# A rebuilt instruction list for a fused attention and feed-forward block: a second mask area, new planned durations, and 117 moved units of work

## The chip, the cores and the metric

The kernel runs on one core of one Trainium2 chip, as one launch. The metric is the device time of that launch in microseconds (us). The core has a matrix engine, TensorE (PE in the profile, with its weight loads listed as PEld), and four others: VectorE (DVE), ScalarE (ACT), GpSimd (POOL) and SyncE (SP). Here SP issues nearly all transfers (DMAs). Every engine works through its own list of instructions in order. An instruction that waits holds up everything behind it on its engine.

## The reference

One transformer block over x[1, 2048, 448], in float32: a pre-LN attention with 16 heads of 28 and a sliding window of 256 keys, then a pre-LN GEGLU feed-forward. The biases and scales of the layer norms are not there.

```python
# attention
qkv = (layernorm(x) @ wqkv).reshape(B, S, 3, 16, 28)...   # q, k, v
scores = einsum("bhqd,bhkd->bhqk", q, k) * 28 ** -0.5
mask = (i - j >= 0) & (i - j < 256)                      # query i, key j
p = softmax(where(mask, scores, -1e9))
h = x + (p @ v) @ wo
# feed-forward, F = 1792
g, u = layernorm(h) @ w_gate, layernorm(h) @ w_up
out = h + (gelu_tanh(g) * u) @ w_down
```

## The kernel before

**Precision.** Projections are computed from operands that are split in a high and a low part (`to_hi`, L435 on ACT; `to_lo`, L438 on DVE or POOL), with several matmul terms summed in PSUM: 11 per 128-row tile of q or k (`project_tile`, L683) and per value tile (`values`, L647), 6 per output tile (`output`, L1001).

**Attention.** The 2048 tokens are 16 tiles of 128. Attention is cut into 16 blocks B = 0 to 15: a block is one group of four heads (B % 4) by one chunk of 512 queries (B // 4). For a block the kernel does two passes over the scores. The first computes scores with queries on the partitions; DVE adds a mask to each piece and takes its maximum (L853). The 32 x 16 maxima of a block are turned on DVE (L883, L885), copied by ACT (L887) and written by four transfers into an extra row of q (`maxima`, L890), so that the second pass gives scores less their maximum. The second pass has keys on the partitions; ACT takes the exponentials (L859) and POOL zeroes what lies outside the window with `affine_select` (L865). Then comes the attention product (`attend`, L939), its scaling (`drain`) with the copies of oblk and ohl on ACT (L435), and the output product (`output`, L1001) with the addition to the residual on DVE (L1004).

PE's matmuls for the two passes are issued in `excursion`: a round of up to 64 small matmuls at a time, of the probabilities of one block, the maxima of another, or both in a row. Each such part writes four of the eight PSUM banks. Between rounds PE does projections, value products, output products, and at the end of attention the first matmuls of the feed-forward (L1243).

**Masks.** A 64-query half tile sees five blocks of 64 keys, of which the first is cut by the window and the last by the diagonal. Those of the first two tiles of the sequence see fewer. For these `tile_keys` returns the list of key blocks of each half and an offset into one mask buffer. Piece x of a tile is computed by one round and has its own mask columns.

**Layer norm and its transposed form.** Each tile is normalised by ACT (L492) into one of two buffers xn. Most tiles of the first norm are transposed on PE. For others, and in the second norm, `turn` transposes within 32 x 32 blocks on DVE (L537) and four SP transfers per tile (L540) carry the result to DRAM, for the first norm to xl and for the second to an xn area there. Its buffer xn in on-chip memory is the same for each of these tiles, so the next tile's transposition writes where these four transfers read. `turned` later loads and splits them.

**Feed-forward.** From about 324 us on a dense stream of half-array matmuls runs (`first` L1243, the gate and up products L1450, the down products L1526 and L1561), each with weight and token splits on ACT, DVE and POOL.

**What sets the order.** No loop order in the source is the order on the chip. Every piece of work is an `Op` of the class `Lists`: engine, cost, latency, a number `key`, what it reads and writes, PSUM banks. `Lists.run` walks through a modelled time. For each engine it looks at the pieces that could start first, within a few hundredths of a microsecond of each other, takes the one with the lowest key, and so appends to that engine's fixed list. The modelled latency of a transfer has an allowance MARGIN. Some elementwise operations have `alts`: the planner picks the engine (ACT or DVE, DVE or POOL) that would end first. So a change of a duration or key changes the orders of all lists, not what is computed.

```python
return min((f for f in found if f[3] <= t0), key=lambda f: (f[1].key, f[0]))[:3]
```

Of the kernel before, what the change touches and what calls it, by code (L numbers as in the profile page):

```python
# [23 lines left out]
BIG = 3.0e38  # L24
# [46 lines left out]
MARGIN = 0.7  # L71
# [24 lines left out]
WARM = 26.0  # L96

# [10 lines left out]
class Op:  # L108
    __slots__ = ("eng", "cost", "lat", "key", "fn", "deps", "users", "left", "banks", "port", "ready", "start", "fin",
# [10 lines left out]
class Lists:  # L120
# [3 lines left out]
    def __init__(self):  # L124
        self.ops, self.seen, self.open, self.all = [], {}, {}, {}
# [171 lines left out]
def block_kernel(ctx: ExitStack, tc, x, wqk_in, wv_in, wo_in, gu_in, rest_in, cw_in, down_in, out):  # L297
# [35 lines left out]
    pool.tile([128, 112], F32, name="pad2")  # L333
# [46 lines left out]
    kept = [m.rearrange("p (b r) -> p b r", r=12) for m in (v_m[:, 8 * VT:8 * VT + 96], mt[:, 512:608])]  # L380
# [59 lines left out]
    def dma(key, size, fn, r=(), w=(), cost=0.44, after=(), tag=None):  # L440
        return op("sp", cost, 0, key, fn, r, w, size=size, after=after, tag=tag)
# [10 lines left out]
    def layer_norms(ts, key, kind):  # L452
# [15 lines left out]

        for t in ts:
# [13 lines left out]
    def normalise(t, key, kind):  # L483
        moved = kind == "ln2" or t in TURNED
# [58 lines left out]
    def turned(t, key, kind):  # L543
        tc = col(t)
# [68 lines left out]
    def constants(after):  # L613
        def const_mask():
            nc.gpsimd.memset(mask, 0.0)
            nc.gpsimd.memset(mask[0:64, 320:384], -BIG)
            for h in HALF[:2]:
# [5 lines left out]
        op("pool", 1.0, 1.0, -18, const_mask, (), ["mask"], port=True, after=after)  # L623
# [7 lines left out]
    def wv_split(p):  # L631
        key = VHALF - 14 if p else WVKEY
# [7 lines left out]
    def values(t, p, n):  # L640
        key = 64 * (t // 4) + (VKEY if t < 12 else VLAST)[t % 4] if t > 3 else 8 * t - 37 if not p else VHALF + 6 * t
# [16 lines left out]
    def wqk_split(m):  # L658
        key = -34 + 3 * m if m < 4 else 6 * m - 28
# [10 lines left out]
    def project_tile(c, m):  # L670
        g, s = divmod(m, 2)
# [99 lines left out]
    def excursion(key, sf, pf):  # L771
        reads, work = [], []
# [49 lines left out]
        for n, (work, reads, writes, width, banks) in enumerate(steps):  # L822
# [3 lines left out]
            cost = width * 4 / 2400 + 0.012  # L826
            ops.append(op("pe", cost, cost + 0.2, key, lambda work=work, banks=banks: run(work, banks), rd, wr, held, tag="bin", mode=3))
# [4 lines left out]
        if sf is not None:  # L832
            banks = steps[-1][4]
# [3 lines left out]
        if pf is not None:  # L837
            width, banks = steps[0][3:]
            for j in range(4):
                probs(key, pf, width, j, banks[j])  # L840
            for G in new:
                select(G, key + 1)
# [31 lines left out]
    def maxima(B):  # L874
        g, u = B % 4, B % 2
# [44 lines left out]
    def attend(B):  # L920
        g, c = block(B)
# [23 lines left out]
        op("pe", cost, cost + 0.2, 16 * B + LAG_V, go, reads, (), banks, tag="att", mode=2)  # L945


    def drain(B):
        (bx, by), h = acc[B], B % 2
# [29 lines left out]
        for cost, fn, rd, wr in steps:  # L979
            cost *= 0.58 if last else 1  # L980
            op(name, cost, cost + 0.05, key + 1, fn, ["oblk", ("rcp", h), *rd], wr, port=True)
        op("dve", 0.625, 0.71, key + 2, lambda: nc.vector.transpose(oT, oblk), ["oblk"], [tok])
# [6 lines left out]
    def output(p, c):  # L989
        B = 4 * c + 2 * p + 1  # L990
        key = 16 * B + LAG_O
        for i in range(4):
            t = c * 4 + i

            k = Bank("last" if B == NB - 1 else "task")
            wk = key + (i if B == NB - 1 else 3 * i)
# [10 lines left out]
    def wo_weights(g):  # L1007
        p, h = divmod(g, 2)
# [94 lines left out]
    def tokens_x(cp, key, parts):  # L1103
# [788 lines left out]
```

## Time and profile before

| what | value |
|---|---|
| time, median of 3 runs | 698.02 us (697.04 to 699.13) |
| the profiled execution's own time | 699.35 us |
| its span (first to last instruction) | 697.6 us |
| granted TensorE clock, mean | 0.998 |
| bytes moved, mean rate | 69.69 MB, 100 GB/s |

The span runs from the first to the last instruction of one profiled execution, and the row of busy times gives each engine's part of it. In a row by stage, what follows the stretch is its length, then for each engine the busy time with the number of instructions that lie in it, then the clock that the throttle granted to TensorE, the share of the DMA engines' time, and the rate. In a row in order of time, the numbers are start and busy time of a group of equal instructions that follow each other, then the engine, the line in the source, the operation, what is written and read, the shape, the count, and in brackets how long the engine stood idle before and on which operation of which engine it waited. In a row of waits, the waiting operation stands left of the arrow and the releaser right, then the sum, the number and the longest of these waits. Matmuls overlap each other in the array, so the busy times of two neighbouring groups overlap by some hundredths of a microsecond.

### The profile page before, as it was taken

The page shows a single profiled execution, that of the slowest core. Times are in us where ns is not written, and L with a number is a line of the kernel's source. Part 1 is how long each engine was busy: PE and PEld are TensorE (multiplying, and loading weights), DVE is VectorE, ACT ScalarE, POOL GpSimd, SP SyncE. Part 2 cuts the span into 40 slices and gives each one's busy share as a digit, 9 for nine tenths or more (in the row PEclk, how much of TensorE's full clock was granted, in tenths as well). Part 3 has the DMA queues.
Part 4 walks back from the last instruction along what each step waited for, and adds up shares of the span by engine and source line. Part 5 has one row for each costly group of instructions (what it writes and reads, how often), then busy time and mean ns, then how long its engine had stood idle before and what let it go on. Part 6 is the DMA issues. An engine that isn't in the chain of part 4 may idle for free. (4 is left out here: it accounts for less than half of the span.)

```text
span 697.6 us, 22824 instructions
## 1 busy us (share of the span) xinstructions
PE 677.0 (97%) x9162; PEld 566.8 (81%) x9162; DVE 525.6 (75%) x1575; ACT 360.8 (52%) x788; POOL 204.6 (29%) x433
## 2 busy tenths in 40 slices
PE   8999999999999989999999999999999999999996
PEld 7887677777876777778988887888889889999885
DVE  8975678767678777638995899676757888887754
ACT  5656646654466464657553465544524544535430
POOL 5335554564546356670210120000000210111000
PEclk9999999999999999999999999999999999999999
DMA  8311211121312426233654666415103744443102
GB/s 306 86 36 40 41 31 55 21 51 31 90 23 55 113 63 216 68 93 110 148 103 128 208 174 193 119 46 142 59 14 119 222 133 132 136 143 86 43 14 106
DMA packets 67081, 69.69 MB, mean 100 GB/s; under 512 B 42528, under 2 KB 55008, under 8 KB 66400
## 3 DMA queue, kind: packets, MB, share of 16 engines
q1 hardware_dynamic: 66832, 68.13, 34.9%
q8 instruction: 71, 1.16, 0.7%
q14 instruction: 34, 0.28, 0.1%
q10 hardware_dynamic: 144, 0.11, 0.0%
HBM read 58.82 MB, written 22.45 MB: 116 GB/s over the span
## 5 line engine op out<-in xcount | busy, mean ns | idle before, releaser
L853 DVE CUSTOM_DVE_ANT_0 mt<-bank,mt 128x64 bf16<-128x64 f32 (+4 forms) x368 | 115.4, 373 | 25.3 <-PE bank L792 22.2
L1450 PE MATMUL bank<-xT,proj 64*128 64x512 f32 x645 | 120.7, 389 | 0.0
L865 POOL TENSOR_SCALAR_AFFINE_SELECT pp<-pp 64x256 f32<-64x256 f32 x240 | 95.9, 418 | 59.8 <-ACT pp L859 54.2
L1450 PE MATMUL bank<-xo,proj 64*128 64x512 f32 x456 | 98.4, 389 | 0.5 <-DVE e L1366 0.3
L859 ACT ACTIVATE pp<-bank 128x512 f32<-128x512 f32 x152 | 78.3, 597 | 24.7 <-PE bank L792 24.2
L1450 PEld LDWEIGHTS bank<-xT,proj 64*128 64x128 f32 x645 | 81.0, 184 | 9.2
L683 PE MATMUL bank<-xT 128*128 128x512 f32 x308 | 80.4, 403 | 2.9 <-ACT pp L859 2.6
L1526 PE MATMUL bank<-proj,gh 64*128 64x448 f32 x624 | 75.3, 363 | 0.3 <-ACT e L1365 0.2
L683 PEld LDWEIGHTS bank<-xT 128*128 128x128 f32 x308 | 55.4, 188 | 19.1 <-ACT pp L859 6.0
L1526 PEld LDWEIGHTS bank<-proj,gh 64*128 64x128 f32 x624 | 63.1, 185 | 6.4 <-ACT e L1365 1.2
L1450 PEld LDWEIGHTS bank<-xo,proj 64*128 64x128 f32 x456 | 59.5, 185 | 8.1 <-DVE e L1366 0.7
L1450 PE MATMUL bank<-xT,w 64*128 64x512 f32 x276 | 53.8, 390 | 0.3 <-DVE raw L1462 0.3
L792 PE MATMUL bank<-k,q 28*64 28x320 f32 (+4 forms) x1624 | 50.1, 331 | 2.2 <-ACT v L435 1.0
L1450 PE MATMUL bank<-xo,w 64*128 64x512 f32 x240 | 49.7, 391 | 0.9 <-DVE raw L1462 0.6
L1545 DVE TENSOR_TENSOR hres<-bank,hres 128x448 f32<-128x448 f32 (+1 forms) x85 | 47.0, 610 | 1.1 <-PE bank L1526 1.1
L647 PE MATMUL bank<-proj,xT 128*128 128x448 f32 (+1 forms) x220 | 44.3, 340 | 1.5 <-ACT pp L859 1.2
L792 PE MATMUL bank<-q,k 29*64 29x192 f32 (+4 forms) x1664 | 44.4, 327 | 0.3 <-DVE mx L853 0.3
L792 PEld LDWEIGHTS bank<-k,q 28*64 28x64 f32 x1624 | 37.3, 131 | 8.1 <-DVE mx L853 2.0
L792 PEld LDWEIGHTS bank<-q,k 29*64 29x64 f32 x1664 | 30.4, 131 | 15.8 <-issue 5.7
L647 PEld LDWEIGHTS bank<-proj,xT 128*128 128x128 f32 x220 | 35.7, 189 | 8.2 <-ACT pp L859 3.1
L939 PEld LDWEIGHTS bank<-pp,v 64*29 64x29 f32 x1664 | 32.1, 103 | 10.8 <-ACT pp L859 3.1
L939 PE MATMUL bank<-pp,v 64*29 64x192 f32 (+4 forms) x1664 | 39.4, 319 | 1.5 <-DVE mx L853 1.2
(197 smaller groups left out, 1297.5 us busy)
## 6 DMA issues: line engine op xcount, KB each, us to landing
gu<-in_gu_dram SPq DMA_DIRECT2D x18, 480.0 KB
proj<-gu SPq DMA_DIRECT2D x24, 288.0 KB
proj<-down SPq DMA_DIRECT2D x22, 224.0 KB
proj<-gu SPq DMA_DIRECT2D x24, 192.0 KB
hres<-in_x_dram SPq DMA_DIRECT2D x16, 224.0 KB
w<-gu SPq DMA_DIRECT2D x12, 288.0 KB
out_dram<-hres SPq DMA_DIRECT2D x15, 224.0 KB
xT<-xn SPq DMA_DIRECT2D x26, 128.0 KB
```

Source lines behind the costliest of these rows:

```text
L647: op("pe", mm(224 * n), 0.29 if n == 1 else 0.38, key + a / 16, lambda a=a, h=h, wb=wb, xb=xb: nc.tensor.matmul(bank[b.k][:, 0:224 * n], x ...
L683: op("pe", mm(512) + 0.002, 0.403, key, lambda a=a, h=h, wb=wb, xb=xb: nc.tensor.matmul(bank[b.k], wqk[m][:, h, wb, :], xT[:, xb, cc * 128 ...
L792: nc.tensor.matmul(bank[banks[j].k][dst, at:at + 64 * n], w, x, start=True, stop=True, tile_position=(32 * j, 64 * h), skip_group_check=True)
L853: nc.vector.tensor_tensor_reduce(junk[turn_of[0]][:, 0:x], bank[b.k][:, 64 * o:64 * o + x], mask[:, lo:lo + x], 1.0, -BIG, OP.add, OP.max, ...
L859: op("act", 0.065 + width * 0.00088, 0.16 + width * 0.00088, key, lambda: nc.scalar.activation(pp[:, j, at:at + width], bank[b.k][:, 0:wid ...
L865: nc.gpsimd.affine_select(a, a, pattern=[[0, 4], [-cm, 64]], compare_op=op_, fill=0.0, base=0, channel_multiplier=cm)
L939: nc.tensor.matmul(bank[banks[h].k][32 * j:32 * j + DH + 1, 64 * lo:64 * hi], v[HALF[h], at_v(4 * c - 2 + kh // 2), 4 * g + j, :], pp[HALF ...
L1450: nc.tensor.matmul(bank[b.k], w, xarea(u.cp, xl, xs, side)[:, xk], start=p in (1, 2, 5) and not k and not t, stop=t == 2, tile_position=(6 ...
L1526: nc.tensor.matmul(bank[banks[q].k][:, 0:D], h[oh][0]()[HALF[x], q * 128:q * 128 + 128], d[wh][0]()[HALF[x]], start=not ph and not y and n ...
L1545: op("dve", 0.07 + w * 0.463 / D, 0.163 + w * 0.463 / D, key, lambda: nc.vector.tensor_tensor(hres[:, t, c0:c0 + w], bank[b.k][:, c0:c0 + ...
```

## The change

**Keys of the first two tiles.** Before, the second half of tiles 0 and 1 had its list of key blocks rotated by one and shared the mask columns by an offset of 64. Now both halves have the same list in ascending order and start at offset 256, and a second diagonal area is added to the mask buffer (at 448 for the lower half, at 512 for the upper), which grows from 384 to 576 columns. Since the halves now agree, adjacent pieces of both can be made by the same matmuls: four score rounds of blocks 0 to 3 have 24 instead of 32 matmuls of their list (32 fewer in all, 1612 for 1644 on this side). The two junk areas move behind the larger mask, and the second half of `kept`, which had lain there, gets a tile of its own in place of the unused `pad2`.

**Planned durations.** In the planner's model MARGIN goes from 0.7 to 0.5, each transfer costs 0.1 more on SP, a score round's first part 0.06 and its last 0.02 in place of 0.012 on top of its columns and its latency 0.28 for 0.2, an attention product's latency 0.42 for 0.2, the mask's construction 1.6 for 1.0.

**Places.** Every unit of work gets a name (`L.unit`: ln for layer norms, x for score rounds, m for the maxima and p for the exponentials of a round, o for output products, q for projections, v for values, and so on), and a table PLACE of 117 entries adds a number to the key of each op of the unit.

No line of the computation changes apart from the first item. As all three change the planner's orders, instructions move on all engines; where an operation has a free choice, nine elementwise additions of the feed-forward go from DVE to POOL. PE has 6653 instructions for 6686, DVE 1569 for 1575, ACT 784 for 787, POOL 444 for 433, SP 558 for 558.

```diff
-MARGIN = 0.7
+MARGIN = 0.5
...
+PLACE = {
+    "k3": -17.1, "kv0": -31, "ln1.4": 18, "q0.0": 6, "kv1": -72, "v3.0": 77, "ln1.5n": 25, "q0.2": -37, "ln1.10": -54,
...
+}
...
-        o.eng, o.cost, o.lat, o.key, o.fn, o.port, o.size, o.tag, o.mode = eng, cost, lat, key, fn, port, size, tag, mode
+        o.eng, o.cost, o.lat, o.fn, o.port, o.size, o.tag, o.mode = eng, cost, lat, fn, port, size, tag, mode
+        o.key, o.unit = key + PLACE.get(self.unit, 0), self.unit
...
-    pool.tile([128, 112], F32, name="pad2")
+    kept_m = pool.tile([128, 112], F32, name="kept")
...
-    mask = mt[:, 0:192].bitcast(BF)
-    junk = [mt[:, 192 + 160 * i:352 + 160 * i].bitcast(BF) for i in range(2)]
+    mask = mt[:, 0:288].bitcast(BF)
+    junk = [mt[:, 288 + 160 * i:448 + 160 * i].bitcast(BF) for i in range(2)]
...
-        return op("sp", cost, 0, key, fn, r, w, size=size, after=after, tag=tag)
+        return op("sp", cost + 0.1, 0, key, fn, r, w, size=size, after=after, tag=tag)
...
     def normalise(t, key, kind):
+        L.unit = f"{kind}.{t}n"
...
     def constants(after):
         def const_mask():
             nc.gpsimd.memset(mask, 0.0)
-            nc.gpsimd.memset(mask[0:64, 320:384], -BIG)
-            for h in HALF[:2]:
+            nc.gpsimd.memset(mask[0:64, 512:576], -BIG)
+            for n, h in enumerate(HALF[:2]):
+                at = 448 + 64 * n
+                nc.gpsimd.affine_select(mask[h, at:at + 64], mask[h, at:at + 64], pattern=[[-1, 64]], compare_op=OP.is_ge,
+                                        fill=-BIG, base=0, channel_multiplier=1)
...
-        op("pool", 1.0, 1.0, -18, const_mask, (), ["mask"], port=True, after=after)
+        op("pool", 1.6, 1.6, -18, const_mask, (), ["mask"], port=True, after=after)
...
     def tile_keys(B, i):
         if block(B)[1] or i > 1:
             return [list(range(2 * i + h, 2 * i + h + 5)) for h in range(2)], 0
-        rows = list(range(4, 2 * i + 6))
-        return [rows, rows[1:] + rows[:1]], 64
+        return [list(range(4, 2 * i + 6))] * 2, 256
...
-            cost = width * 4 / 2400 + 0.012
-            ops.append(op("pe", cost, cost + 0.2, key, lambda work=work, banks=banks: run(work, banks), rd, wr, held, tag="bin", mode=3))
+            cost = width * 4 / 2400 + (0.06 if not n and len(steps) > 1 else 0.02)
+            ops.append(op("pe", cost, cost + 0.28, key, lambda work=work, banks=banks: run(work, banks), rd, wr, held, tag="bin", mode=3))
...
-        op("pe", cost, cost + 0.2, 16 * B + LAG_V, go, reads, (), banks, tag="att", mode=2)
+        op("pe", cost, cost + 0.42, 16 * B + LAG_V, go, reads, (), banks, tag="att", mode=2)
```

Line numbers grow by 17 to 47: the maxima L853 are now L883, the exponentials L859 are L889, the maxima's four transfers L890 are L921, normalisation L492 is L511, the transposition L537 is L556 and its transfers L540 are L559, copies L435 are L452, the attention product L939 is L971, the output product L1001 is L1036, the feed-forward's L1243 is L1284.

How instructions moved is shown at three places, each as the rows of one engine's list, before and then with the change.

SP's list around the four transfers of the first transposed tile of the first norm (xl<-xn). L693/L720 and L696/L723 carry keys of the projection, L890/L921 are the maxima's transfers, L1057 loads wo. Before:

```order
L890 DMA q_160<-mt 1x4x128 x4
L540 DMA xl_136<-xn 32x14x32 x2
L693 DMA k_157<-k_154 4x512 x4
L540 DMA xl_136<-xn 32x14x32 x2
L696 DMA k_154<-k_157 4x512
L693 DMA k_157<-k_155 4x512 x4
L540 DMA xl_137<-xn 32x14x32 x4
```

and with the change:

```order
L559 DMA xl_136<-xn 32x14x32 x3
L921 DMA q_159<-mt 1x4x128 x4
L1057 DMA raw<-in_wo_dram 128x448
L720 DMA k_157<-k_156 4x512 x4
L559 DMA xl_136<-xn 32x14x32
L723 DMA k_156<-k_157 4x512
L720 DMA k_157<-q_158 4x512 x4
L921 DMA q_160<-mt 1x4x128 x4
L559 DMA xl_137<-xn 32x14x32 x4
```

The first tile's four transfers were split in two and two by four key copies; now they stand as three and one, with nine transfers of three other kinds in between. The next tile's four stay together in both.

ACT's list in the middle of attention: pp<-bank are exponentials of a probability round, oblk the copy of an attention product, q and k the copies of a projection, mt<-mt the copies of the maxima. Before:

```order
L859 ACTIVATE pp<-bank_144 128x512
L492 ACTIVATE xn<-hres,bnve 128x448
L887 ACTIVATE mt<-mt 32x32 x4
L435 ACTIVATE oblk<-bank_143 128x512
L435 ACTIVATE k_154<-bank_141 128x512
L492 ACTIVATE xn<-hres,bnve 128x448
L859 ACTIVATE pp<-bank_140 128x512
L859 ACTIVATE pp<-bank_142 128x512
```

and with the change:

```order
L889 ACTIVATE pp<-bank_146 128x512
L511 ACTIVATE xn<-hres,bnve 128x448
L452 ACTIVATE q_159<-bank_140 128x512
L889 ACTIVATE pp<-bank_141 128x512
L889 ACTIVATE pp<-bank_142 128x512
L889 ACTIVATE pp<-bank_144 128x512
L889 ACTIVATE pp<-bank_145 128x512
L511 ACTIVATE xn<-hres,bnve 128x448
L452 ACTIVATE k_156<-bank_141 128x512
L889 ACTIVATE pp<-bank_142 128x512
```

The second normalisation stood directly ahead of the exponentials of a round; with the change a projection's copy stands between each of the two and the exponentials that follow.

PE's list at the end of attention, from the last attention product to the last output product. Before:

```order
L939 MATMUL bank_144<-pp,v 29x128
L1243 MATMUL bank_143<-xT,proj 128x512
L1243 MATMUL bank_142<-xT,proj 128x512
...
L1243 MATMUL bank_142<-xT,proj 128x512
L1001 MATMUL bank_145<-proj,ohl 128x448 x5
L1001 MATMUL bank_145<-proj 128x448
```

with 24 rows of L1243 in all, and with the change:

```order
L971 MATMUL bank_145<-pp,v 29x128
L1284 MATMUL bank_142<-xT,proj 128x512
L1284 MATMUL bank_143<-xT,proj 128x512
...
L1284 MATMUL bank_142<-xT,proj 128x512
L1036 MATMUL bank_145<-proj,ohl 128x448 x5
L1036 MATMUL bank_145<-proj 128x448
```

with 48 rows of L1284. So 24 more matmuls of the feed-forward stand between the two products.

On DVE the number of maxima L853 between consecutive transpositions L537 changes. The 12 turned tiles of the two norms that lie in attention come in three groups of four, with three gaps each: 12, 16, 12; 8, 20, 8; 8, 12, 8 maxima before, and 20, 20, 20; 12, 8, 12; 20, 8, 20 with the change.

More of the change, by code (lines that the diff above doesn't have):

```diff
@@ L108 @@
 class Op:
-    __slots__ = ("eng", "cost", "lat", "key", "fn", "deps", "users", "left", "banks", "port", "ready", "start", "fin",
+    __slots__ = ("eng", "cost", "lat", "key", "fn", "deps", "users", "left", "banks", "port", "ready", "start", "fin", "unit",
                  "size", "tag", "mode", "alts", "then", "soft")
@@ L124, in __init__ @@
     def __init__(self):
-        self.ops, self.seen, self.open, self.all = [], {}, {}, {}
+        self.ops, self.seen, self.open, self.all, self.unit = [], {}, {}, {}, None
     def op(self, eng, cost, lat, key, fn, r=(), w=(), bank=None, port=False, size=0, tag=None, after=(), part=None, mode=0, alts=None):
```

32 lines of the change are left out of this document (31 added, 1 removed), and 13 rows, old and new, of the table PLACE.

## The prediction

> **What bounds the kernel now.** First the page's busy times:
>
> ```profile
> PE 677.0 (97%) x9162; PEld 566.8 (81%) x9162; DVE 525.6 (75%) x1575; ACT 360.8 (52%) x788; POOL 204.6 (29%) x433
> ```
>
> Then the same by stage (start, attention, feed-forward): stretch, its length, busy time of PE, PEld, DVE, ACT and POOL, clock, DMA share and GB/s.
>
> ```profile
> 0.00:28.00 28.00, 25.17 (x172) 21.50 (x175) 23.96 (x57) 16.77 (x31) 16.13 (x45) 1.00 0.68 226
> 28.00:325.00 297.00, 286.95 (x5710) 224.02 (x5696) 215.41 (x953) 168.53 (x360) 153.10 (x343) 1.00 0.24 63
> 325.00:692.00 367.00, 364.93 (x3303) 321.27 (x3300) 285.16 (x565) 175.53 (x399) 35.35 (x45) 1.00 0.43 118
> ```
>
> PE is the bound throughout. Its idle time is 2.83 us in the start, 10.05 us in attention (297.00 less 286.95), 2.07 us in the feed-forward and 5.6 us after its last matmul at 692.0. The granted clock is 1.00 in all three stages, so no matmul gets faster. A new list can win only what PE waits, so I next read who PE waits for between 27 and 325 us: the sum, the number of waits and the longest, of the two entries on exponentials (L859).
>
> ```profile
> PE bank L683 <- ACT pp L859: 2.6, 5, 0.9
> PE bank L647 <- ACT pp L859: 1.2, 1, 1.2
> ```
>
> No single engine is short of time (ACT 57% busy, DVE 73% there). The waits are for PSUM banks that ACT or DVE release late. The order of time shows why; each row below is one instruction group, with its engine's idle time and releaser at the end.
>
> ```profile
> 73.02 0.65 DVE L537 STREAM_TRANSPOSE xn<-xn 128x448 f32<-128x448 f32 x1 [2.21 <-DMA xl<-xn]
> 74.74 1.12 PE L792 MATMUL bank<-q,k 29*64 29x320 f32 x32
> 76.46 1.12 PE L792 MATMUL bank<-k,q 28*64 28x320 f32 x32 [0.60 <-DVE mx L853]
> 78.24 1.21 PE L683 MATMUL bank<-xT 128*128 128x512 f32 x4 [0.66 <-ACT pp L859]
> ...
> 135.93 0.65 DVE L537 STREAM_TRANSPOSE xn<-xn 128x448 f32<-128x448 f32 x1 [0.93 <-DMA xn<-xn]
> 136.70 0.76 ACT L492 ACTIVATE xn<-hres,bnve 128x448 f32<-128x448 f32 x1 [1.16 <-DVE xn L537]
> 137.36 2.04 ACT L859 ACTIVATE pp<-bank 128x512 f32<-128x512 f32 x4
> 137.99 2.81 PE L683 MATMUL bank<-xT 128*128 128x512 f32 x11 [0.90 <-ACT pp L859]
> ...
> 156.04 0.65 DVE L537 STREAM_TRANSPOSE xn<-xn 128x448 f32<-128x448 f32 x1 [2.00 <-DMA xn<-xn]
> 157.49 1.08 PE L1001 MATMUL bank<-wos,ohl 128*128 128x448 f32 x4 [0.56 <-DVE mx L853]
> ...
> 201.11 0.76 ACT L492 ACTIVATE xn<-hres,bnve 128x448 f32<-128x448 f32 x1 [1.23 <-POOL bnve L467]
> 202.40 1.08 PE L647 MATMUL bank<-proj,xT 128*128 128x448 f32 x4 [1.24 <-ACT pp L859]
> ```
>
> The transpose of a normalised tile (L537) writes the buffer that the four transfers of the tile before still read. It waits for them at the head of DVE's list, the maxima behind it come late, the next normalisation (L492) on ACT waits for the transpose, and the exponentials (L859) behind that one release PE's bank late. The normalisations and these transposes, standing in front of other work, account for 0.60 + 0.66 + 0.90 + 0.56 + 1.24 = 3.96 us of PE's 10.05. The largest other single wait is at the end of attention:
>
> ```profile
> 314.90 3.01 PE L1243 MATMUL bank<-xT,proj 64*128 64x512 f32 x24
> 317.84 0.88 PE L1001 MATMUL bank<-proj,ohl 128*128 128x448 f32 x3
> 319.79 0.68 PE L1001 MATMUL bank<-proj,ohl 128*128 128x448 f32 x2 [1.07 <-ACT ohl L435]
> ```
>
> The last output product stands 24 matmuls behind the last attention product, and its input is 1.07 us late.
>
> **The change part by part.** Matmul for matmul the work is the same, but for 32 fewer score matmuls and one warm-up transpose fewer. From about 324 us in the old time PE's list runs on identically.
>
> Removed matmuls: in blocks 0 to 3 a score round of 32 instructions (64 records) becomes one of 24 (48 records), four times.
>
> ```profile
> 65.70 1.43 PE L792 MATMUL bank<-k,q 28*64 28x128 f32 x64
> 67.06 2.79 PE L683 MATMUL bank<-xT 128*128 128x512 f32 x11
> 69.78 1.12 PE L792 MATMUL bank<-q,k 29*64 29x128 f32 x48
> ...
> 83.12 1.12 PE L792 MATMUL bank<-q,k 29*64 29x128 f32 x48
> 84.04 1.23 PE L792 MATMUL bank<-k,q 28*64 28x128 f32 x48
> 85.20 2.58 PE L683 MATMUL bank<-xT 128*128 128x512 f32 x10
> ```
>
> From start to next start the long round takes 67.06 - 65.70 = 1.36 us and the short one 85.20 - 84.04 = 1.16, which is 0.20 less. The bounds are 0 (the columns streamed are the same) and 0.20 each; I take 0.15: 4 x 0.15 = **-0.6 us**.
>
> Added switches: the two orders cut PE's list into stretches of one array layout (full array, score tiles, attention tiles, half rows). Up to the dense feed-forward there were 119 and are now 128. What one costs shows where eleven L683 matmuls run in one piece (67.06 to 69.78 above, 2.72 us), against 5 and 6 around an attention product:
>
> ```profile
> 142.77 1.43 PE L683 MATMUL bank<-xT 128*128 128x512 f32 x5
> 144.13 2.56 PE L939 MATMUL bank<-pp,v 64*29 64x192 f32 x112
> 146.62 1.67 PE L683 MATMUL bank<-xT 128*128 128x512 f32 x6
> 148.22 1.12 PE L792 MATMUL bank<-q,k 29*64 29x128 f32 x48
> ```
>
> 1.36 + 1.60 = 2.96, so 0.24 for one more piece with two ends, 0.12 an end. Nine more stretches cost 9 x 0.12 = **+1.1 us**; the upper bound is the whole piece each, 9 x 0.24 = 2.2, the lower one 0. [...]
>
> The end of attention: 48 instead of 24 matmuls now stand between the last attention product and the last output product, 3 us more cover for an input that was 1.07 us late. The 24 come from earlier in the same part, so nothing is added. The next thing that could be late is the last attention product itself, which has about the same work ahead of it after its last score round as before. **-1.1 us** (0 to -1.3).
>
> The transposes: four of nine gaps within their three groups of four waited. The orders have 12, 16, 12; 8, 20, 8; 8, 12, 8 maxima (L853) between consecutive transposes, and now 20, 20, 20; 12, 8, 12; 20, 8, 20. The page's row on them:
>
> ```profile
> L853 DVE CUSTOM_DVE_ANT_0 mt<-bank,mt 128x64 bf16<-128x64 f32 (+4 forms) x368 | 115.4, 373 | 25.3 <-PE bank L792 22.2
> ```
>
> At a mean of 373 ns eight more are 3.0 us, four more 1.5. That covers the gap that ended at 73.02 (2.21) and the one at 135.93 (0.93), and most of that at 156.04 (2.00). On ACT, by the new order, no normalisation stands directly ahead of exponentials; in between stands a projection's copy, which waits for eleven matmuls (2.72 us) anyway. So of the 3.96 us I count 1.26, 0.90, half of 0.56 and three quarters of 1.24 as gone, 3.4. Against this, one gap fell from 20 maxima to 8, and such gaps waited up to 2.00 us on DVE; I charge 0.5. **-2.9 us**, bounds -4.0 and, by the slower rival below, +5.0.
>
> The other waits: 10.05 - 3.96 - 1.07 = 5.0 us, spread over a dozen places. Two rounds that stood back to back now have eleven matmuls between them, several output products are cut into pieces of five and six that fill short gaps, and maxima copies often stand behind the first exponential, whose bank PE needs. But ten pairs of rounds still have only a projection between them, and static order moves waits as well as removes them. I take a third: **-1.6 us**, bounds 0 and -5.0. A wait also costs a restart: from the probability round at 74.74 to the score round at 76.46 are 1.72 us, where the undisturbed pair at 83.12 and 84.04 takes 0.92, so 0.20 are lost beyond the 0.60 counted. I take 0.1 for each of eight waits, **-0.8 us**.
>
> The start and the mask: POOL has two selects (0.23 us each) and a wider memset more, at about 10 us.
>
> ```profile
> 10.42 0.23 POOL L618 TENSOR_SCALAR_AFFINE_SELECT mt<-mt 64x64 bf16<-64x64 bf16 x1
> 15.91 0.23 POOL L459 TENSOR_SCALAR bnve<-bnmv 128x2 f32<-128x2 f32 x1 [4.11 <-DVE bnmv L472]
> ```
>
> POOL is idle for 4.11 us right behind, so this costs nothing; without that cover, about 0.7 us. The loads and value products in the first 28 us are reordered, with PE's amount of work within 1.1 us: 0, between -0.6 and +0.6. In the feed-forward nine additions move from DVE to POOL, which is idle there (35.35 of 367 us): 0, between -1 and +1.
>
> Sum: -0.6 + 1.1 - 1.1 - 2.9 - 1.6 - 0.8 = -5.9 us, on the span 697.6 -> 691.7. The profiled execution took 699.35 with what lies around the span, 1.33 above the median of 698.02; the difference goes on the median: **692.1 us**. With the bounds of the terms short of a loss, this case spans 689 to 695.5.
>
> **The rivals.** *All waits go*: the list was rebuilt with later arrivals for transfers and bank releases, so each producer may now be in time. All 10.05 us, 1.9 of restarts (19 waits at 0.1) and 0.6, less 1.1: -11.5, 686.5 us. Against it: the ten tight pairs. *The waits move*: only the end and the matmuls are won, the switches are paid, and the waits form elsewhere: -0.6 - 1.1 + 1.1 and a little, about 697.4 us. For it: the same engines, and producers fixed in order. *The feed-forward takes it back*: DVE has 0.87 us idle in 40 there, so its token and weight splits set the pace once PE comes earlier.
>
> ```profile
> 320.00:360.00 40.00, 39.63 (x329) 35.83 (x330) 39.13 (x78) 29.34 (x64) 4.99 (x10) 1.00 0.58 133
> ```
>
> Much of that chain starts with the last output's additions and so moves along with PE, which speaks against it. If 3.4 of the 5.9 us return as waits in the feed-forward, 2.5 stay won: 695.5 us. *Slower, by SP's queue*: tile 12's four transfers now stand as three, then four of the maxima, one weight load and four key copies, then the last one; five of the twelve tiles are split so, against two. If that last piece lands after the DVE work in between is done, each split tile costs PE what the wait at 73.02 did, 0.60 + 0.66: 5 x 1.26 = 6.3 us, on top of 2.7 of the old waits that stay, against 3.96 now: +5.0. With -0.6, -1.1 and +1.1 the time is 702.4 us. It decides where nine queued transfers take longer than the twenty maxima put in between.
>
> **How the numbers follow.** Forecast 0.58; all waits go 0.09; waits move 0.15; feed-forward takes it back 0.10; SP's queue 0.08. A difference under 0.3% (2.1 us) can't be told from none here. Faster holds the forecast, the first rival and half of the third: 0.58 + 0.09 + 0.05, and a little of the second, 0.73; same 0.18; slower 0.09. The range leaves out the slower rival and the far end of the first: 686.8 to 698.8.
>
> **What would show it.** The transposes of normalised tiles should start without DVE idle before them, PE's attention waits should fall from 10 to about 5 us, the last output product should run without a break, and the dense feed-forward should begin near 318.7 us and last as long as now from its first row:
>
> ```profile
> 324.56 2.50 PE L1243 MATMUL bank<-xT,w 64*128 64x512 f32 x18
> ```
>
> I am wrong if PE's waits for exponentials stay above 3 us, if the waits in the feed-forward grow beyond 3 us, or if the start is later by a microsecond.

## The result and the profile after

The changed kernel takes 688.30 us (median of 4 runs, 686.89 to 688.50) against 698.04 us (697.04 to 699.13) for the kernel before in the same runs: a ratio of 0.9856, with a 95% interval of 0.9836 to 0.9875. That is 9.7 us less. The forecast was 692.1 us, 5.9 less.

The profiled execution took 688.24 us with a span of 686.5. Its busy times, then three stretches (0 to 28 us, from there to the dense feed-forward, and from there to PE's last group of matmuls):

```profile
PE 673.7 (98%) x9097; PEld 564.5 (82%) x9097; DVE 526.9 (77%) x1569; ACT 361.7 (53%) x785; POOL 218.2 (32%) x444
...
0.00:28.00 28.00, 25.76 (x150) 22.62 (x151) 23.79 (x54) 14.49 (x28) 15.52 (x43) 1.00 0.69 231
28.00:313.03 285.03, 283.14 (x5646) 220.43 (x5645) 216.63 (x955) 171.09 (x362) 154.65 (x347) 1.00 0.24 64
313.03:679.20 366.17, 362.00 (x3290) 319.06 (x3289) 282.62 (x553) 176.13 (x397) 48.01 (x54) 1.00 0.43 118
```

The stretches of the kernel before that end at the same places in the program, which the prediction did not need:

```profile
28.00:324.56 296.56, 286.51 (x5707) 223.58 (x5692) 214.97 (x952) 168.09 (x359) 153.10 (x343) 1.00 0.24 63
324.56:689.15 364.59, 362.59 (x3289) 319.28 (x3288) 282.75 (x560) 175.97 (x400) 35.35 (x45) 1.00 0.43 117
```

From these rows the span can be taken apart without a rest:

| part | before | after | difference |
|---|---|---|---|
| PE idle, first 28 us | 2.83 | 2.24 | -0.6 |
| PE idle, 28 us to the dense feed-forward | 10.05 | 1.89 | -8.2 |
| PE busy, up to the dense feed-forward | 311.68 | 308.90 | -2.8 |
| dense feed-forward to PE's last group | 364.59 | 366.17 | +1.6 |
| from there to the end of the span | 8.45 | 7.30 | -1.15 |
| span | 697.6 | 686.5 | -11.1 |

In the last part all instructions of the two profiles stand at the same distances, and only the last transfers end earlier. The profiled execution of before lay 1.33 us above its median, that of the change at its median, so this 1.15 is likely part of what one execution differs from the next, and not of the 9.7.

The waits of PE from 28 us to the dense part, after:

```profile
PE bank L819 <- issue: 1.6, 2, 1.4
PE bank L819 <- DVE raw L1009: 0.2, 1, 0.2
```

Of 19 waits above 0.15 us three are left, and none is for exponentials or maxima. The largest, for which the profile names no releaser, took 1.39 us here and between 0.14 and 1.12 us in later profiles of the same list up to that place. In order of time, the transpositions of the first group and the end of attention:

```profile
51.39 0.64 DVE L556 STREAM_TRANSPOSE xn<-xn 128x448 f32<-128x448 f32 x1
63.48 0.63 DVE L556 STREAM_TRANSPOSE xn<-xn 128x448 f32<-128x448 f32 x1
75.00 0.63 DVE L556 STREAM_TRANSPOSE xn<-xn 128x448 f32<-128x448 f32 x1
86.61 0.60 DVE L556 STREAM_TRANSPOSE xn<-xn 128x448 f32<-128x448 f32 x1
...
299.72 2.55 PE L971 MATMUL bank<-pp,v 64*29 64x192 f32 x112
302.20 5.75 PE L1284 MATMUL bank<-xT,proj 64*128 64x512 f32 x48
307.89 1.29 PE L1036 MATMUL bank<-proj,ohl 128*128 128x448 f32 x5
...
309.22 1.19 PE L1036 MATMUL bank<-proj,ohl 128*128 128x448 f32 x5
...
310.46 1.19 PE L1036 MATMUL bank<-proj,ohl 128*128 128x448 f32 x5
...
313.03 2.34 PE L1284 MATMUL bank<-xT,w 64*128 64x512 f32 x18
```

No transposition, of this group or the others, has DVE idle ahead of it, and the last output products run without a break, though the transfers of the first transposed tile stand split in SP's list. In the feed-forward, by contrast, PE's waits grow from 1.8 to 4.1 us, and three are new:

```profile
344.93 1.54 PE L1573 MATMUL bank<-proj,xT 64*128 64x448 f32 x12 [1.38 <-DVE e L1411]
373.49 0.50 PE L1497 MATMUL bank<-xo,w 64*128 64x512 f32 x2 [0.86 <-ACT v L1503]
447.16 0.73 PE L1497 MATMUL bank<-xo,proj 64*128 64x512 f32 x3 [1.04 <-DVE raw L1509]
```

### The profile page after: what moved, and what is told of

Its sections match the earlier page's. It is cut to its first block, busy times and chain, and to the rows that moved or that the text cites. A ratio compares the mean times of both kernels' runs of the same rounds, so it can differ in the third digit from the quotient of the medians.

```text
span 686.5 us, 22714 instructions
## 1 busy us (share of the span) xinstructions
PE 673.7 (98%) x9097; PEld 564.5 (82%) x9097; DVE 526.9 (77%) x1569; ACT 361.7 (53%) x785; POOL 218.2 (32%) x444
## 3 DMA queue, kind: packets, MB, share of 16 engines
q8 instruction: 71, 1.16, 0.7%
## 5 line engine op out<-in xcount | busy, mean ns | idle before, releaser
L883 DVE CUSTOM_DVE_ANT_0 mt<-bank,mt 128x192 bf16<-128x192 f32 (+4 forms) x368 | 115.5, 373 | 24.2 <-PE bank L819 23.4
L889 ACT ACTIVATE pp<-bank 128x512 f32<-128x512 f32 x152 | 79.4, 599 | 25.2 <-PE bank L819 25.1
L819 PE MATMUL bank<-k,q 28*64 28x320 f32 (+4 forms) x1560 | 47.8, 336 | 0.4 <-DVE raw L1009 0.2
L1410 ACT ACTIVATE e<-bank 1x1 f32<-1x1 f32 x78 | 12.3, 157 | 54.2 <-PE bank L1573 41.1
L1573 PE MATMUL bank<-proj,xT 64*128 64x448 f32 x312 | 38.0, 364 | 1.6 <-DVE e L1411 1.4
```

The costliest lines, as they stand in the source:

```text
L819: nc.tensor.matmul(bank[banks[j].k][dst, at:at + 64 * n], w, x, start=True, stop=True, tile_position=(32 * j, 64 * h), skip_group_check=True)
L883: nc.vector.tensor_tensor_reduce(junk[turn_of[0]][:, 0:x], bank[b.k][:, 64 * o:64 * o + x], mask[:, lo:lo + x], 1.0, -BIG, OP.add, OP.max, ...
L889: op("act", 0.065 + width * 0.00088, 0.16 + width * 0.00088, key, lambda: nc.scalar.activation(pp[:, j, at:at + width], bank[b.k][:, 0:wid ...
L1410: ways = {"act": (0.08, 0.17, lambda: nc.scalar.activation(e8[0:1, 0:1], bank[b.k][0:1, 0:1], AF.Copy), False), "dve": (0.07, 0.17, lambda ...
L1573: nc.tensor.matmul(bank[banks[q].k][:, 0:D], h[oh][0]()[HALF[x], q * 128:q * 128 + 128], d[wh][0]()[HALF[x]], start=not ph and not y and n ...
```

## The experiments

Line numbers in rows of an experiment are those of its own file. Where a kernel keeps a given list, the planner's result was recorded and the instructions written out in that order, with the stated ones moved; each engine's list is otherwise the same, row for row. "Idle" is PE's, from 28 us to the dense feed-forward.

**The three parts, each alone or left out.** First the mask, on the kernel before; its lists stay as they were.

```diff
-        rows = list(range(4, 2 * i + 6))
-        return [rows, rows[1:] + rows[:1]], 64
+        return [list(range(4, 2 * i + 6))] * 2, 256
```

> The kernel before with the second mask area alone; its lists are the same as before but for 32 fewer score matmuls and the two selects. My theory (a round of 48 records takes 0.15 us less than one of 64, four times, and nothing else moves): 0.6 us less, about 697.4, PE's waits in attention stay at 10 us. Rival (fewer matmuls in a round also shorten the score rounds elsewhere or remove waits, since the score rounds of the changed kernel took about 2 us less in all): about 696.

Measured: 701.44 us (median of nine), ratio 1.0043 (1.0028 to 1.0058, without one execution of 710.34 us), so slower by 0.4%, where both readings had it faster. The round itself does what was said:

```profile
65.40 1.23 PE L794 MATMUL bank<-k,q 28*64 28x128 f32 x48
66.55 2.80 PE L686 MATMUL bank<-xT 128*128 128x512 f32 x11
```

From start to start 1.15 us where the 64 records took 1.36, so 0.21 less. Laid beside the profile of before matmul by matmul, PE is 0.5 us ahead at 67 us, 1.2 at 76 (a wait of 0.60 is gone), 1.9 at 141, then 0.6 at 230, and at 276 it is 0.5 behind, at the end 0.7. A wait of 0.56 us at 157 us has become 1.22, and one of 0.58 is new at 276 us. A PE that comes earlier finds others later, so single waits move. By sum they do not grow, though: 9.8 us against 10.0. The 0.8 us that four such rounds should win are lost elsewhere, 0.4 in the first 28 us by a longer wait at 8 us, and the rest in small steps while PE works. The larger loss of the timed runs, 2.6 us by their medians, comes up below with the clock.

Second, the planned durations alone, on the kernel before (the first diff, with the other durations); third, the change with an empty table (the second diff); fourth, the change with the old durations (the first diff taken back).

```diff
-MARGIN = 0.7
+MARGIN = 0.5
...
-        return op("sp", cost, 0, key, fn, r, w, size=size, after=after, tag=tag)
+        return op("sp", cost + 0.1, 0, key, fn, r, w, size=size, after=after, tag=tag)
```

```diff
 PLACE = {
-    "k3": -17.1, "kv0": -31, "ln1.4": 18, "q0.0": 6, "kv1": -72, "v3.0": 77, "ln1.5n": 25, "q0.2": -37, "ln1.10": -54,
...
 }
```

> The kernel before with the new planned durations alone. Theory A (the waits went because the table moves transposes and normalisations away from what PE waits for): without the table the waits stay, PE idle between 28 us and the dense feed-forward 8 to 11 us, time 696 to 699. Theory B (the planner knew transfers and bank releases too early, and with the right durations each producer is in time by itself): PE idle there below 4 us, time 690 to 692.

> The changed kernel with an empty table, that is durations and mask. Theory A: 0.6 us below the run with the durations alone, 695.5 to 698.5, all of the rest of the 9.8 us belongs to the table. Theory B: 689.5 to 691.5, the table is worth 1 to 3 us.

> The changed kernel with the old durations, that is table and mask. Theory A (the places by themselves carry the gain): PE idle in attention stays below 4 us, time 688 to 691. Theory B (the durations carry it): waits of 6 us or more come back, 694 to 698. A third reading (the table's numbers are offsets that fit only one modelled time, so that with other durations they scatter the work at random): as slow as before or slower, 697 to 704.

| kernel | time, us | ratio (95%) | idle, us | at work, us |
|---|---|---|---|---|
| before | 698.83 | | 10.0 | |
| mask | 701.44 | 1.0043 (1.0028 to 1.0058) | 9.8 | +0.3 |
| durations | 701.39 | 1.0038 (1.0022 to 1.0053) | 8.4 | +4.2 |
| durations and mask | 701.04 | 1.0030 (1.0014 to 1.0046) | 7.4 | +3.0 |
| table and mask | 699.04 | 1.0005 (0.9994 to 1.0015) | 7.0 | +3.2 |
| all three | 688.30 | 0.9856 (0.9836 to 0.9875) | 1.8 | -2.9 |

"At work" is the time from each of PE's groups to the next without the idle time between them, summed over attention and the feed-forward matmuls at full array height (L1255), against before. Idle here is the sum of the waits in the rows. The 688.30 us of the last row were timed beside other runs of before, with a median of 698.04.

Theory B falls with the second and third run: the durations alone leave 8.4 us of waits. Theory A had the waits of the durations alone right, but both runs were slower than it said (696 to 699 and 695.5 to 698.5). It falls with the fourth: with the places and the old durations 7.0 us are left, 3.9 of them in four waits for exponentials. The third reading of that run has its time right, as slow as before; that the places then scatter the work at random was not shown. Of these kernels only the one with all three takes the waits away. Places and durations without the mask were not run, nor was the table alone, so that the mask is needed is not shown.

**Where the single parts lose more than they wait.** The column "at work" says that PE was also slower while it worked. The rows around the longest wait in attention of the run with the durations alone, in order of time and then by stretch:

```profile
301.96 1.12 PE L792 MATMUL bank<-q,k 29*64 29x128 f32 x48
305.27 5.28 PE L1255 MATMUL bank<-xT,proj 128*128 128x512 f32 x15 [2.19 <-ACT pp L859]
...
302.52:305.93 3.41, 1.23 (x35) 0.88 (x20) 1.66 (x3) 2.31 (x5) 1.24 (x3) 1.00 0.40 135
305.93:309.34 3.41, 3.41 (x10) 2.63 (x9) 1.43 (x2) 1.56 (x3) 3.16 (x9) 0.50 0.00 0
309.34:312.76 3.42, 3.42 (x117) 2.93 (x116) 1.54 (x2) 0.00 (x0) 0.52 (x1) 1.00 0.02 5
```

After the wait of 2.19 us the granted clock is 0.50 for 3.41 us, by an estimate from these two numbers 1.7 us on top of the wait. The same stands behind a wait of 2.19 us in the runs with an empty table, where fifteen matmuls take 5.31 us, and with the old durations, where nine take 3.90 (nine take 2.35 at 268.77 us of the run with the durations alone). The durations alone have one more such stretch, at 111 us: 21 matmuls of L647 take 6.03 us, where eleven take 2.39 at 100.67. So of the 4.2, 3.0 and 3.2 us "at work" about 0.8, 1.3 and 1.5 have another cause, which stays open. By kind of group, summed in the same way, the score rounds take 2.1, 2.1 and 1.2 us more in these three, 0.1 more with the mask alone and 2.2 less with all three. Two runs were made to see when this happens: into the changed kernel's dense feed-forward 16 waits were put, by transpositions that need a chain of GpSimd operations. Single executions took 773.70 and 756.37 us, at mean clocks of 0.960 and 0.966.

```diff
+            nc.tensor.transpose(bank[b.k][:, 0:128], ident, ident)
+            for _ in range(n):
+                nc.gpsimd.affine_select(ident, ident, pattern=[[1, 128]], compare_op=OP.is_ge, fill=0.0, base=0,
+                                        channel_multiplier=1)
+            nc.tensor.transpose(bank[b.k][:, 0:128], ident, ident)
             go()
```

> The changed kernel with 16 waits put into PE's list in the dense feed-forward, from about 0.5 to 4 us long, two of them as close pairs of short ones. Theory A (a wait of about 2 us, or two within that time, halves PE's granted clock for 3.5 us soon after, and one below 1.4 us does not): half clock for 3 to 4 us behind each wait above 2 us, none behind those below 1.2. Theory B (the dips seen in the single-part kernels have to do with what PE does there and not with the waits): no dips in the dense part. [...]

> As the run with 16 waits, with waits of 1.1 to 2.6 us alone. [...] If the length of the wait alone decides, one length divides those with from those without.

The close pairs of the first run did not come about (their waits lie 12 and 8 us apart). Two waits of the second run, with the clock around them:

```profile
581.36 0.33 PE L1943 MATMUL bank<-ident 128*128 128x128 f32 x1 [1.86 <-POOL ident L1941]
597.23 0.35 PE L1943 MATMUL bank<-ident 128*128 128x128 f32 x1 [2.00 <-POOL ident L1941]
...
593.99:597.40 3.41, 1.41 (x12) 0.76 (x8) 2.53 (x7) 0.76 (x2) 1.70 (x5) 1.00 0.46 134
597.40:600.82 3.42, 3.42 (x17) 2.71 (x18) 0.00 (x0) 0.36 (x1) 0.35 (x1) 0.50 0.00 0
576.92:580.34 3.42, 2.57 (x23) 1.98 (x19) 2.18 (x5) 1.68 (x5) 0.63 (x3) 1.00 1.03 344
580.34:583.75 3.41, 2.40 (x21) 2.05 (x23) 1.11 (x2) 0.00 (x0) 0.83 (x3) 1.00 0.16 60
```

Behind the wait of 2.00 us the granted clock is 0.50 for 3.42 us, here in the dense part, against the first run's theory B. Around the one of 1.86 us it is 1.00, from 576.92 to 583.75 us. In the run with the durations alone a wait of 2.63 us ahead of 461.16 us is followed by no such stretch: the twelve matmuls of L1526 at 464.04 take 1.37 us, like the twelve at 457.16 ahead of it. In the run on transpositions below, a wait of 1.66 us comes with one: the clock is 0.50 from 204.78 us on, after 1.34 us of it. So the length of a wait alone does not decide, against the first run's theory A: no one length divides 1.66 and 2.00 from 1.86 and 2.63. What decides was not shown.

The stretch at 111 us of the run with the durations alone comes with two waits, of 0.95 and 0.49 us, ahead of 109.89 and 111.46. Single waits of 1.24 us (before, ahead of 202.40) and of 1.39 (the changed kernel, ahead of 268.74) have a clock of 1.00 behind them. The eight executions of the mask alone that are compared had mean clocks of 0.994 to 1.000 and spans of 698.0 to 702.1 us, the profiled one at 0.998 and 698.0 the shortest. The clock can be a part of its loss, but not the whole: one execution at a mean clock of 1.000 took 699.7 us. Only the profiled one has a trace, so the rest stays open. In the profiles of before and after the clock is 0.50 only behind PE's last matmul, from 695.17 us (it ends at 691.93) and from 686.84 us (681.98), so it has no part in the difference of these two.

**The transpositions.** On the list of before, with PE's list left as it is:

```diff
+            while n < [20,20,20,16,20,16,12,12,12][turns.index(one) - g // 4]:
+                i += 1
+                n += dve[i].src == "most"
+            dve.insert(i + 1, two)
...
+            while not (act[i - 1].src == "probs" and act[i].src != "probs"):
+                i += 1
+            act.insert(i, norm)
...
+            sp[i:i] = four
```

Each transposition stands behind 20, 16 or 12 maxima from the one before it (12, 16, 12; 8, 20, 8; 8, 12, 8 before), its four transfers in one piece behind it, and its normalisation behind the four exponentials of a round and not ahead of them. What loads and splits a moved tile moves later with it.

> The kernel before with one thing moved: the transpositions of normalised tiles stand at least 12 to 20 maxima apart, each with its four transfers in one piece behind, and the normalisations stand behind a round's exponentials; PE's list is the same. My theory (the 3.96 us of waits come from these standing in front of other work): PE idle in attention falls from 10 to 6.5 to 7 us, time about 695. Rival (the waits move to the next late producer): idle 9 to 10 us, time 697 to 699.

Measured: 703.27 us, ratio 1.0067 (1.0051 to 1.0084), idle 9.9 us. At the first place the term holds, with only a wait of 0.33 left of 0.60 and 0.66:

```profile
74.70 1.12 PE L840 MATMUL bank<-q,k 29*64 29x320 f32 x32
75.61 1.07 PE L840 MATMUL bank<-k,q 28*64 28x320 f32 x32
77.01 1.19 PE L731 MATMUL bank<-xT 128*128 128x512 f32 x4 [0.33 <-ACT pp L907]
```

PE's row at 78.24 of before now starts at 77.01, 1.23 us earlier (0.60 + 0.66 were counted). But in the third group a worse wait arises, shown here on ACT, DVE and PE:

```profile
201.00 2.06 ACT L907 ACTIVATE pp<-bank 128x512 f32<-128x512 f32 x4 [0.50 <-PE bank L840]
202.93 0.78 ACT L540 ACTIVATE xn<-hres,bnve 128x448 f32<-128x448 f32 x1
...
203.74 0.65 DVE L585 STREAM_TRANSPOSE xn<-xn 128x448 f32<-128x448 f32 x1 [3.16 <-ACT xn L540]
...
205.10 3.95 PE L987 MATMUL bank<-pp,v 64*29 64x320 f32 x110 [1.66 <-DVE mx L901]
...
204.78:208.19 3.41, 3.08 (x73) 2.33 (x80) 2.63 (x16) 0.61 (x3) 0.73 (x2) 0.50 0.40 70
```

The normalisation, put behind the exponentials, is now itself late; the transposition waits 3.16 us for it at the head of DVE's list, the maxima behind it come late, PE waits 1.66 us, and the clock is 0.50 for 3.41 us. Between 201.7 and 209.0 us PE loses 3.9 us against before. So the chain that the prediction named is real, and it works in both directions; moving its links by hand in a list that is otherwise kept moves the wait. The distance by itself did what it was meant to do: in before, four transpositions within the groups wait for transfers of xn (2.21, 0.93, 2.00 and 0.96 us), here none does. But five now wait for their normalisation, from 0.30 to 3.16 us, and the distance without that move was not run. The rival of this run is nearer, and the time is worse than either.

**The end of attention.** The change with 24 of the 48 matmuls moved behind the last output products:

```diff
+    pe[first - 4:first + 24] = outs + pe[first - 4:first]
```

> The changed kernel with 24 of the 48 feed-forward matmuls ahead of the last output products put behind them. My theory: the wait of about 1.1 us of before comes back at that place, and the dense part starts 1.1 us later. Rival (the input is early by itself in the new order): no wait, the same time.

```profile
300.75 3.02 PE L1332 MATMUL bank<-xT,proj 64*128 64x512 f32 x24
303.69 0.88 PE L1084 MATMUL bank<-proj,ohl 128*128 128x448 f32 x3
305.72 0.67 PE L1084 MATMUL bank<-proj,ohl 128*128 128x448 f32 x2 [1.16 <-ACT ohl L500]
...
310.50 3.02 PE L1332 MATMUL bank<-xT,proj 64*128 64x512 f32 x24
313.36 0.39 PE L1332 MATMUL bank<-xT,w 64*128 64x512 f32 x1
315.26 2.33 PE L1332 MATMUL bank<-xT,w 64*128 64x512 f32 x17 [1.52 <-DVE hres L1087]
```

A single execution took 690.23 us. The wait comes back with 1.16 us, as the theory has it. And it costs more than itself: the 24 matmuls of the output take 310.50 - 303.69 = 6.81 us, without a wait they take 313.03 - 307.89 = 5.14 (rows of after above), so 0.51 us are lost beyond the 1.16. The same 0.51 stands in before (324.56 - 317.84 - 1.07 = 5.65). So from the last attention product (298.26 here, 299.72 in the changed kernel) to the first row of the dense part it is 1.79 us longer, where 1.1 was expected. Behind it a next wait of 1.52 us shows what the outputs release.

**Changes of the layout.** The last four output products with 6 feed-forward matmuls, out of the 48, between each two:

```diff
+    pe[first - 3:first + 24] = parts[0] + cover[0:1] + parts[1] + cover[1:2] + parts[2] + cover[2:3] + parts[3]
```

> The changed kernel with its last four output products cut apart by 6 feed-forward matmuls each, taken from the 48 ahead of them: three more pieces, six more changes of the array layout. My price (0.12 us an end): the stretch from the last attention product to the dense part takes 0.7 us more, beyond a wait of up to 0.5 us ahead of the first output product, which has 30 matmuls of cover. Upper bound of the forecast (0.24 an end): 1.4 us more. Rival (a change of layout costs nothing of its own): 0 to 0.2.

```profile
299.18 2.55 PE L1019 MATMUL bank<-pp,v 64*29 64x192 f32 x112
...
306.69 0.67 PE L1084 MATMUL bank<-proj,ohl 128*128 128x448 f32 x2 [0.51 <-ACT ohl L500]
...
308.72 1.29 PE L1084 MATMUL bank<-proj,ohl 128*128 128x448 f32 x5
...
310.15 0.96 PE L1332 MATMUL bank<-xT,proj 64*128 64x512 f32 x6
311.04 1.29 PE L1084 MATMUL bank<-proj,ohl 128*128 128x448 f32 x5
...
313.35 1.28 PE L1084 MATMUL bank<-proj,ohl 128*128 128x448 f32 x5
...
314.77 2.75 PE L1332 MATMUL bank<-xT,w 64*128 64x512 f32 x18
```

A single execution took 690.14 us. An output product and six matmuls take 311.04 - 308.72 = 2.32 us and the next 2.31. Uncut they take 310.46 - 309.22 = 1.24 and 5.69 / 8 = 0.71 (302.20 to 307.89), so 1.95. Two ends cost 0.37 us, 0.18 each: between the forecast's 0.12 and 0.24, and the rival of no cost falls. From the last attention product to the dense part the run takes 314.77 - 299.18 = 15.59 us against 13.31 in the changed kernel. Less the wait of 0.51 that is 1.77 us more, above the expected 0.7 and its bound of 1.4: six ends at 0.18 are 1.1, and most of the rest stands again behind the wait, around the first output product: it takes 2.51 us to the matmuls that follow it, where the next takes 310.15 - 308.72 = 1.43.

**The feed-forward.** The change up to the last output product, and behind it the lists of ACT, DVE, POOL and SP of before:

```diff
+    L.order = early + [by[n] for n, _, _ in rows]      # rows: the late part of the recorded list of before
```

> The changed kernel up to the last output product; behind it each engine's list, engine choices and PSUM banks of the kernel before (PE's list is the same in both). Theory A (the changed order of ACT, DVE, POOL and SP in the feed-forward costs the 2.4 us of waits that it has more): PE idle there falls from 4.1 to about 1.8 us, time about 686. Theory B (PE reaches the feed-forward 11 us earlier and its weights and tokens are late by themselves): idle 4 us or more, time 688 to 690.

> The changed kernel again, beside the next run on the same chip: 687.5 to 689 by its first times, no half clock before the last matmul.

> The changed kernel with the feed-forward order of the kernel before, again. If the changed feed-forward order costs what the waits show: 1.5 to 2.5 us less than the run beside it, 686 to 687. If the first difference was one of chips or days: the same within 0.5 us.

The waits of PE from the dense part on, in the first of these:

```profile
PE bank L1654 <- DVE raw L1666: 0.9, 2, 0.6
PE bank L1730 <- DVE e L1568: 0.7, 1, 0.7
PE bank L1730 <- ACT e L1567: 0.5, 1, 0.5
PE bank L1654 <- DVE e L1568: 0.3, 1, 0.3
```

They come to 2.5 us against 4.1 (in the second pair 2.5 against 4.6), so 1.6 to 2.1 of the 2.4 us that the feed-forward had more are the order's, and the rest comes with the earlier start. The three new waits are gone, others of 0.75 and 0.52 us stand in their place. By time the hybrid took 686.66 us (ratio to before 0.9834, 0.9821 to 0.9846) at first, and the second time 686.25 (0.9820, 0.9807 to 0.9834) beside 686.80 (0.9839, 0.9820 to 0.9857) for the change, which was somewhat below the 687.5 expected of it, with no half clock before PE's last matmul in its profile (mean clock 0.999). That is 0.55 us less where 1.5 to 2.5 were expected, and the intervals overlap: that the hybrid beats the changed kernel is not shown.

## Why the prediction was right, and where it was not

The sign, the cause and the range held; the size of the gain was 5.9 us where 9.7 came. By time the rival *all waits go* (686.5 us) lay nearer to the measured 688.30 than the forecast did. Part of the hit is luck: terms that were too small on the winning side (restarts, other waits) met losses that were taken too small or as nothing (switches, feed-forward). By its steps:

- **Bound and stages.** PE was the bound, and most of what came off was its waits. That a new list can win only what PE waits was too narrow: PE's busy time up to the dense part fell by 2.8 us as well. The dense part began at 313.03 where "near 318.7" was forecast, without the rival's loss by SP's split transfers: no transposition waited.
- **Removed matmuls, -0.6.** 0.21 us a round measured against 0.15 taken. Alone it did not show in the time, which rose.
- **Switches, +1.1.** The price of an end is 0.18 us at the one pair of layouts measured, above the 0.12 taken. Nine more stretches are nine more ends, so by this price they would cost 9 x 0.18 = 1.6 us, an estimate, within the upper bound of 2.2. Yet PE's busy time fell by 2.8, so other terms outweighed it.
- **Restarts, -0.8.** This term was mis-sized. It took 0.1 us for each of eight waits. The output products show 0.51 us beyond the wait itself, twice, but these are dear ones. Over all waits between 28 us and the dense part, the step from the matmul ahead of a wait to the one behind it, less the idle time and less what the same pair of shapes usually takes in these traces, comes to about 3 us for the 19 waits of before and 0.7 for the three of after. That is an estimate of about 0.15 us a wait and 2.3 us for the 16 that went. With -0.8 for the removed matmuls and +1.6 for the switches it makes -1.5 of the 2.8 us, and the other 1.3 stay open; by kind of group the largest fall is in the score rounds (2.2 us, the removed matmuls among them).
- **The end of attention, -1.1.** Right: the wait comes back with 24 matmuls of cover, and the break is gone with 48.
- **Transpositions, -2.9.** The chain was right (1.23 us of 1.26 at the first place), and in the changed kernel no transposition waits. Whether the larger distance wins this by itself is not shown: when it was set by hand no transposition waited for transfers any more, but the normalisations that were moved with it came late, and the kernel was 4.7 us slower.
- **Other waits, -1.6.** Too small: the step "I take a third" failed. All but 1.9 of 10.05 us went. The rival *all waits go* had this at a chance of 0.09, with "each producer may now be in time" as its ground. What told against it, the ten tight pairs of rounds, did not wait.
- **The start and the feed-forward, 0.** The start won 0.6. The feed-forward lost 1.6, so the rival *the feed-forward takes it back* happened beside the forecast, by three new waits that are mostly the changed order's. PE's waits there came to 4.1 us, so of the prediction's signs of being wrong the one on waits in the feed-forward beyond 3 us came, read as their total; their growth was 2.4. That this part lasts as long as before did not hold.
- **What was not thought of.** With a wait of 2.19 us the clock was 0.50 for 3.41 us, by estimate 1.7 us more. It is not in the difference of the two profiles, but it is part of why parts of the change that had fewer waits were slower than before, and the price of the rival *slower* would have had to hold it.

Most errors were of one kind: the sum went term by term, as if each wait had a cause of its own that an edit takes away. By these runs the waits of a static list hang together. The parts that were run alone or in pairs made the kernel 0 to 3 us slower; all three made it 9.7 us faster. What remains open is which of the 117 places matter, and whether the mask is needed; every edit of the table redraws the whole list.

## What to carry to other kernels

Judge a rebuilt static order as a whole, by its own trace: parts of it tried alone can have the opposite sign, and a gain at one place of a fixed list was lost again further on in both lists that were otherwise kept here. When pricing a wait of the engine that sets the time, count the restart with it (here about 0.15 us on average, 0.5 at the output products) and a possible stretch at half clock: here 0.50 for 3.41 or 3.42 us came with waits of 1.66, 2.00 and 2.19 us, and none with 1.39, 1.86 and 2.63.

## What the runs showed of the hardware that was not expected

Some waits of PE cost more than their length here. With a wait of 2.19 us (the durations alone, ahead of 305.27 us) the granted clock was 0.50 for 3.41 us, with one of 2.00 (the second run with waits put in, ahead of 597.23) 0.50 for 3.42, and with one of 1.66 (the transpositions, ahead of 205.10) 0.50 for 3.41. No half clock came with waits of 1.39 us (the changed kernel, ahead of 268.74), 1.86 (the second run with waits put in, ahead of 581.36) and 2.63 (the durations alone, ahead of 461.16). So in these runs the length alone did not tell whether the estimated 1.7 us would come on top. How much of the spread between executions this makes was not measured.
